# A spectral filter and a gated MLP summed on one core: another layout for the filtered products, and another route for the final sums

## The chip, the core and the metric

The kernel runs on one core of a Trainium2 chip. A core has a matrix engine (TensorE, PE in the profile, with its weight loads shown apart as PEld), a vector engine (VectorE, DVE), a scalar engine (ScalarE, ACT), a general engine (GpSimd, POOL) and a queue that only issues transfers here (SyncE, SP). They run side by side and wait for each other through semaphores. On-chip data lie in SBUF (128 partitions); TensorE writes its results to PSUM, eight banks of 512 float32 per partition, from which VectorE or ScalarE must copy them before a bank can be used again. The metric is the device time of one execution in microseconds (us).

## The reference

```python
x  = A_x                                   # 1 x 2048 x 640, bf16
xn = layernorm(x)
# A: spectral filter
X  = rfft2(xn.astype(float32))             # over 2048 and 640
yA = irfft2(X * (w_r + 1j * w_i), s=(2048, 640)).astype(bf16)   # w: 2048 x 321
# B: gated MLP without a nonlinearity
g  = xn @ w_gate                           # 640 -> 1536
u  = xn @ w_up
yB = (g * u) @ w_down                      # 1536 -> 640
out = x + yA + yB
```

## The kernel before

A small list scheduler in the kernel orders tasks for every engine ahead of time, with estimates of their durations; each engine then runs a fixed list in order, with semaphore waits between the lists. TensorE has three long stages in a row: the products g and u (L978 and L998 in the profile) interleaved first with the forward transform along 2048, then with the filter, and at the end the product with w_down (L1237).

**The filter.** There are 32 steps q. In each, a matmul (L1079, "C") finishes the forward transform of a group of rows into a PSUM bank; VectorE multiplies it by the real and by the imaginary part of the filter weights ("WM": two instructions of L1094 and one of L1097); another engine makes a negated copy of one half ("NG": L1106 on ScalarE, L1107 on VectorE or GpSimd); GpSimd arranges the rest ("NS": L1114 to L1116); ten matmuls ("IA": L1130 and L1131) take 128-column slices of these products as their weights and start the inverse transform. The frequencies are treated in classes, k = 0 to 3 for those of a residue modulo 10 and its mirror (h), and a fifth for the multiples of 5.

```python
# WM: psum (k h m) times weights (m k, ten apart), for the real and the imaginary weights (w)
for h in range(2):
    xh = ps[:, bk, 0:256].rearrange("p (k h m) -> p h m k", k=4, h=2)[:, h]
    wv = wg[:, :, 0:320].rearrange("p w (m k) -> p w m k", k=10)
    wv = wv[:, :, :, 1:5] if h == 0 else wv[:, :, :, 9:5:-1]
    dst = yg[:, 578:1090].rearrange("p (w h m k) -> p h w m k", w=2, h=2, k=4)[:, h]
    c.e.tensor_tensor(dst, xh.unsqueeze(1).to_broadcast([128, 2, 32, 4]), wv, _OP.mult)   # L1094
...
# NG: negated copy of the imaginary products
yg[:, 322:578]  <-  -1.0 * yg[:, 834:1090]
...
# IA
for k in range(5):
    if k < 4:
        l1, l2 = yg[:, 578 + k:1090:4], yg[:, 322 + k:834:4]
    else:
        l1, l2 = yg[:, 0:128], yg[:, 128:256]
    dst = ps[:, bk, 64 * k:64 * k + 64]
    c.e.matmul(dst, l1, v_ti[:, q, 0, :], start=True, stop=False)        # L1130
    ins = c.e.matmul(dst, l2, v_ti[:, q, 1, :], start=False, stop=True)  # L1131
# eIA: 320 sums from PSUM to SBUF, on ScalarE or VectorE (L718 / L719)
```

In the products' buffer the four classes k lie next to each other, element by element: VectorE writes them in one run, and the 128 columns that TensorE loads as weights for one class are four elements (8 bytes) apart.

**The end.** For each of 16 row tiles a, in two halves of 320 columns, twelve matmuls with w_down (L1237) and one that closes the inverse transform (L1249, "IV") add up in one PSUM bank. Beside it, for each pair of tiles, five small matmuls per tile ("I", L1159), a copy from PSUM, and a chain of thirteen VectorE instructions ("V", L1183 to L1216) prepare what IV multiplies. Then:

```python
def em_f1(c, ...):      # FIN, L1257: PSUM + residual -> output buffer, bf16
    return c.e.tensor_tensor(v_out[:, a % 2, sl3], ps[:, bk, 0:320], v_xr[:, xs, sl3], _OP.add)
f1 = T("FIN_%d_%d" % (a, hf), "dve", ..., frees=own, after=[iv])      # frees the bank
dma("st_out%d_%d" % (a, hf), ov[:, a, sl3], v_out[:, a % 2, sl3], ...) # a store per half
```

The last tile is cut in three (320, 192, 128 columns). The small copies that ScalarE and VectorE share (L718, L719) are one helper, so one line has many shapes.

Of the kernel before, what the change touches and what calls it, by code (L numbers as in the profile page):

```python
# [495 lines left out]
_ACTF = mybir.ActivationFunctionType  # L496
# [28 lines left out]
def _d_dve_psum(n):  # L525
    return n * 1.04 + 82.0
# [24 lines left out]
def _build(nc, A_x, A_w_r, A_w_i, B_w_gate, B_w_up, B_w_down, out, opts=None):  # L551
# [3 lines left out]
    with es:  # L555
# [147 lines left out]
        def bank_of(t):  # L703
            return t.units[1]
# [321 lines left out]
        for t in range(16):  # L1026
# [46 lines left out]
            for g in range(2):  # L1073
                q = 2 * t + g
                pg = pq + 0.0005 * g
                ys = 2 * yr + g

                def em_c(c, q=q, g=g, ar=ar):
                    return c.e.matmul(ps[:, bank_of(c.t), 0:_LP], v_tf[:, q, :], v_a[:, ar, 324 * g:324 * g + _LP],  # L1079
                                      start=True, stop=True)  # L1080
                tc = T("C_%d" % q, "pe", _d_mm(_LP), em_c, reads=[(b_a, ("r", 2 * ar, 2 * ar + 2)), (b_tf, ("t", t, t + 1))],
                       prio=pg, bank="single", cls="b")

                def em_wm(c, tc=tc, yr=yr, wr=wr, q=q, g=g):
                    bk = bank_of(tc)
                    o_ = 321 * (q % _WQ)
                    wg = v_wr[wr][:, :, o_:o_ + 321]
                    yg = v_y[:, yr, g]
                    for h in range(2):
                        xh = ps[:, bk, 0:256].rearrange("p (k h m) -> p h m k", k=4, h=2)[:, h]  # L1090
                        wv = wg[:, :, 0:320].rearrange("p w (m k) -> p w m k", k=10)
                        wv = wv[:, :, :, 1:5] if h == 0 else wv[:, :, :, 9:5:-1]
                        dst = yg[:, 578:1090].rearrange("p (w h m k) -> p h w m k", w=2, h=2, k=4)[:, h]
                        c.e.tensor_tensor(dst, xh.unsqueeze(1).to_broadcast([128, 2, 32, 4]), wv, _OP.mult)  # L1094
                    x5 = ps[:, bk, 256:321].unsqueeze(1).to_broadcast([128, 2, 65])
                    d5 = yg[:, 0:512].rearrange("p (w n) -> p w n", w=2)[:, :, 0:65]
                    return c.e.tensor_tensor(d5, x5, wg[:, :, 0:321:5], _OP.mult)  # L1097
                wm = T("WM_%d" % q, "dve", 895.0, em_wm,
                       reads=[(b_wr[wr][0], ("r", b_wr[wr][1], b_wr[wr][1] + 16))],
                       writes=[(b_y, ("r", 4 * ys, 4 * ys + 1))], prio=pg - 0.001, frees=tc)  # L1100
                hold(tc, wm)

                def em_ng(c, yr=yr, g=g):
                    yg = v_y[:, yr, g]
                    if c.e is nc.scalar:
                        return c.e.activation(yg[:, 322:578], yg[:, 834:1090], _ACTF.Copy, scale=-1.0)  # L1106
                    return c.e.tensor_scalar(yg[:, 322:578], yg[:, 834:1090], -1.0, None, _OP.mult)  # L1107
                T("NG_%d" % q, opts.get("ng_eng", ('pool', 'act', 'dve')),
                  {"act": _d_act(256), "dve": _d_dve_ts16(256), "pool": 900.0}, em_ng,
                  reads=[(b_y, ("r", 4 * ys, 4 * ys + 1))], writes=[(b_y, ("r", 4 * ys + 1, 4 * ys + 2))], prio=pg - 0.001)  # L1110

                def em_ns(c, yr=yr, g=g):
                    yg = v_y[:, yr, g]
                    c.e.tensor_copy(yg[:, 65:128], yg[:, 257:320])  # L1114
                    c.e.tensor_copy(yg[:, 193:256], yg[:, 1:64])  # L1115
                    return c.e.tensor_scalar(yg[:, 128:193], yg[:, 256:321], -1.0, None, _OP.mult)  # L1116
                T("NS_%d" % q, "pool", 700.0, em_ns,
                  reads=[(b_y, ("r", 4 * ys, 4 * ys + 1))], writes=[(b_y, ("r", 4 * ys + 2, 4 * ys + 3))], prio=pg - 0.001)

                def em_ia(c, q=q, yr=yr, g=g):  # L1120
                    bk = bank_of(c.t)
                    ins = None
                    yg = v_y[:, yr, g]
                    for k in range(5):
                        if k < 4:
                            l1, l2 = yg[:, 578 + k:1090:4], yg[:, 322 + k:834:4]
                        else:
                            l1, l2 = yg[:, 0:128], yg[:, 128:256]
                        dst = ps[:, bk, 64 * k:64 * k + 64]
                        c.e.matmul(dst, l1, v_ti[:, q, 0, :], start=True, stop=False)  # L1130
                        ins = c.e.matmul(dst, l2, v_ti[:, q, 1, :], start=False, stop=True)  # L1131
                    return ins
                ia = T("IA_%d" % q, "pe", 10 * _d_mm(64), em_ia,
                       reads=[(b_y, ("r", 4 * ys, 4 * ys + 3)), (b_wd, ("e", 128 * q, 128 * q + 128))],
                       prio=pg, bank="single", cls="b")

                def em_eia(c, ia=ia, t=t, g=g):
                    src = ps[:, bank_of(ia), 0:320].rearrange("p (k a m) -> p k a m", k=5, a=16)
                    return copy_on(c, v_z2w[:, :, :, t, 4 * g:4 * g + 4], src)
                eia = T("eIA_%d" % q, ("act", "dve"), {"dve": _d_dve_psum(320), "act": _d_act(320)}, em_eia,  # L1140
                        writes=[(b_z2, ("t", q, q + 1))], prio=pg - 0.001, frees=ia)
                hold(ia, eia)
# [78 lines left out]
        for a in range(16):  # L1221
# [5 lines left out]
            for hf, (c0, c1) in enumerate(pieces):  # L1227
                rb = [("r", 640 * (a % 2) + c0, 640 * (a % 2) + c1)]
                sl3 = slice(c0, c1)
                cuts = (0, 5, 9, 12) if a < opts.get("acc_split", 16) else (0, 12)  # L1230
                own = ag2 = None
                for k0, k1 in zip(cuts[:-1], cuts[1:]):
                    def em_ag2(c, a=a, sl3=sl3, k0=k0, k1=k1, own=own):
                        bk = bank_of(c.t) if own is None else bank_of(own)
                        ins = None
                        for ft in _FT_ORDER[k0:k1]:
                            ins = c.e.matmul(ps[:, bk, 0:sl3.stop - sl3.start], v_ht[:, ft, a * 128:(a + 1) * 128],  # L1237
                                             v_wd[:, ft, sl3], start=(ft == _FT_ORDER[0]), stop=False)
                        return ins
                    kw = dict(bank="single", cls="acc") if own is None else dict(after=[ag2])  # L1240
                    fts = _FT_ORDER[k0:k1]
                    rd = [(b_wd, ("e", 640 * min(fts), 640 * (max(fts) + 1)))] if k1 - k0 < 12 else [(b_wd, None)]
                    ag2 = T("ACC_%d_%d_%d" % (a, hf, k0), "pe", (k1 - k0) * _d_mm(c1 - c0), em_ag2,
                            reads=[(b_ht, ("col", a, a + 1))] + rd,
                            prio=pc + 0.01 + 0.001 * hf + opts.get("acc0_prio", 0.0) * (a < opts.get("acc_split", 16)), **kw)
                    own = own or ag2

                def em_iv(c, own=own, a=a, sl3=sl3):
                    return c.e.matmul(ps[:, bank_of(own), 0:sl3.stop - sl3.start], v_sm[:, 2, :], v_v[:, a, sl3],  # L1249
                                      start=False, stop=True)  # L1250
                iv = T("IV_%d_%d" % (a, hf), "pe", _d_mm(c1 - c0), em_iv,
                       reads=[(b_v, ("a", a, a + 1)), (b_sm, ("t", 1, 3))],
                       prio=opts.get("iv_prio", 5.0) + 0.05 * a + 0.01 + 0.001 * hf, after=[ag2])

                def em_f1(c, own=own, a=a, xs=xs, sl3=sl3):
                    bk = bank_of(own)
                    return c.e.tensor_tensor(v_out[:, a % 2, sl3], ps[:, bk, 0:sl3.stop - sl3.start], v_xr[:, xs, sl3],  # L1257
                                             _OP.add)
                f1 = T("FIN_%d_%d" % (a, hf), "dve", _d_dve_psum(c1 - c0), em_f1,
                       reads=[(b_xr, ("r", xs, xs + 1))], writes=[(b_out, rb[0])],  # L1260
                       prio=opts.get("fin_prio", 41.0) + 0.05 * a - 0.001, frees=own, after=[iv])
                dma("st_out%d_%d" % (a, hf), ov[:, a, sl3], v_out[:, a % 2, sl3], 128 * 2 * (c1 - c0), [],
                    prio=pc - 0.003, reads=[(b_out, rb[0])], semkey=("out", a % 2, hf))

        sch.window = 100.0
        sch.urgent = opts.get("urgent", ('T0_0', 'T0_1', 'T0_2', 'T0_3', 'sd_1', 'sd_2', 'sd_3'))
# [83 lines left out]
```

## Time and profile before

| | |
|---|---|
| time, median of 3 runs | 204.33 us (204.27 to 204.45) |
| span of the profiled execution | 202.8 us |
| granted TensorE clock in every stretch asked for | 1.00 |
| final sums on VectorE (L1257, 320 columns) | 31 times, 483 ns each |
| copies by ScalarE of 128x320 from PSUM | 25 times, 436 ns each |
| products of the filter (L1094) | 64 times, 416 ns each |
| stores of the output | 31, of 80 KB in the median |

How to read it: the profile gives each engine's busy time in us and as a share of the span, and groups instructions by line, shapes and engine. A duration is that of one instruction from start to end; neighbours overlap, so the distance from one start to the next is shorter (the two L1094 of a step take 0.76 us together, not 0.83). TensorE's matmul ends are modelled, so a busy TensorE is not proof of a full one: distances between starts are the better measure. "Idle before" names the engine whose semaphore ended a wait.

### The profile page before, as it was taken

How to read it: one execution, taken by the hardware profiler on the slowest of the kernel's cores; microseconds unless marked ns; L12 is line 12 of the kernel's file. 1: busy time of each engine (PE TensorE's matmuls, PEld its weight loads, DVE VectorE, ACT ScalarE, POOL GpSimd, SP SyncE). 2: the span in 40 equal slices, each digit the busy share in tenths (PEclk: the TensorE clock that was granted, in tenths of full speed). 3: DMA queues.
4: the chain of work that ended last, by engine and by line, in shares of the span. 5: the costliest groups of instructions: out<-in, count | busy, mean ns of one | idle time of the engine just before them, and what ended most of it. 6: DMA issues, size and time to landing. Idle time of an engine off the chain costs nothing.

```text
span 202.8 us, 4769 instructions
## 1 busy us (share of the span) xinstructions
PE 198.0 (98%) x1785; PEld 128.1 (63%) x1785; DVE 179.5 (89%) x511; ACT 127.5 (63%) x277; POOL 32.0 (16%) x108
## 2 busy tenths in 40 slices
PE   7999999999999999899999999999999999999995
PEld 7987644454444555556666666667777767777774
DVE  3599999999999997697988898864999999999983
ACT  3678899999975776869999999987611220200000
POOL 0000000000000000075754675453000000000000
DMA  6999983031161597605354444004313332332222
GB/s 183 300 341 378 377 80 65 3 65 32 32 63 39 112 276 194 197 14 132 74 145 114 103 102 127 0 5 136 92 32 97 106 107 66 113 90 81 93 65 65
DMA packets 31542, 23.82 MB, mean 117 GB/s; under 512 B 10528, under 2 KB 29472, under 8 KB 31392
## 3 DMA queue, kind: packets, MB, share of 16 engines
q1 hardware_dynamic: 30720, 23.16, 43.5%
q10 hardware_dynamic: 800, 0.36, 0.6%
q8 instruction: 14, 0.23, 0.5%
q14 instruction: 8, 0.07, 0.1%
HBM read 18.92 MB, written 2.62 MB: 106 GB/s over the span
## 4 chain that ended last, share of the span: by engine, by line
PE 85%; DVE 5%; SPq 4%; DMA 4%; issue 1%; ACT 1%
PE ps L978 44%; PE ps L1237 23%; SPq L712 4%; DMA arena<-in_A_x_dram 4%; PE ps L1131 3%; PE ps L1130 3%; PE ps L998 2%; PE ps L1079 2%; PE ps L938 2%; PE ps L1159 2%; PE ps L1249 2%; PE ps L1056 2%; DVE arena L719 1%; DVE arena L1257 1%; DVE arena L1186 0%
## 5 line engine op out<-in xcount | busy, mean ns | idle before, releaser
L718 ACT ACTIVATE arena<-ps 128x512 bf16<-128x512 f32 (+7 forms) x206 | 104.8, 547 | 40.1 <-PE ps L1159 24.0
L978 PE MATMUL ps<-arena 128*128 128x512 bf16 x420 | 97.0, 379 | 0.1
L978 PEld LDWEIGHTS ps<-arena 128*128 128x128 bf16 x420 | 38.9, 98 | 41.9 <-ACT arena L718 1.4
L1237 PE MATMUL ps<-arena 128*128 128x320 bf16 (+2 forms) x396 | 56.5, 295 | 0.2 <-DVE arena L1257 0.2
L1237 PEld LDWEIGHTS ps<-arena 128*128 128x128 bf16 x396 | 37.6, 98 | 13.9 <-DVE arena L1257 0.5
L1094 DVE TENSOR_TENSOR arena<-ps,arena 128x256 bf16<-128x256 f32 x64 | 24.0, 416 | 0.1
L1014 DVE TENSOR_TENSOR arena<-arena 128x512 bf16<-128x512 bf16 x42 | 17.7, 421 | 4.7 <-ACT arena L718 4.7
L1107 POOL TENSOR_SCALAR arena<-arena 128x256 bf16<-128x256 bf16 x8 | 6.8, 855 | 89.3 <-DVE arena L1097 89.2
L719 DVE CAST arena<-ps 64x321 bf16<-64x321 f32 (+1 forms) x25 | 12.2, 490 | 6.3 <-PE ps L1131 5.8
L1257 DVE TENSOR_TENSOR arena<-ps,arena 128x320 bf16<-128x320 f32 (+2 forms) x33 | 15.4, 473 | 1.8 <-PE ps L1249 1.8
L998 PE MATMUL ps<-arena 128*128 128x128 bf16 (+1 forms) x160 | 14.4, 246 | 0.4 <-ACT arena L718 0.4
L1130 PEld LDWEIGHTS ps<-arena 128*128 128x128 bf16 x160 | 12.4, 114 | 2.8 <-ACT arena L718 0.4
L998 PEld LDWEIGHTS ps<-arena 128*128 128x128 bf16 x160 | 12.0, 98 | 2.1 <-ACT arena L718 1.2
L1130 PE MATMUL ps<-arena 128*128 128x64 bf16 x160 | 13.3, 196 | 0.0
L1131 PE MATMUL ps<-arena 128*128 128x64 bf16 x160 | 13.3, 197 | 0.0
L1131 PEld LDWEIGHTS ps<-arena 128*128 128x128 bf16 x160 | 11.2, 113 | 2.1
L1116 POOL TENSOR_SCALAR arena<-arena 128x65 bf16<-128x65 bf16 x32 | 12.1, 378 | 0.0
L1114 POOL COPY arena<-arena 128x63 bf16<-128x63 bf16 x32 | 8.6, 268 | 17.1 <-DVE arena L1097 17.0
L1097 DVE TENSOR_TENSOR arena<-ps,arena 128x130 bf16<-128x130 f32 x32 | 9.3, 292 | 0.0
L776 ACT ACTIVATE arena<-arena 128x640 bf16<-128x640 bf16 x11 | 9.1, 824 | 0.0
L1115 POOL COPY arena<-arena 128x63 bf16<-128x63 bf16 x32 | 9.0, 280 | 0.0
L891 DVE TENSOR_TENSOR arena<-arena 128x384 f32<-128x384 bf16 x16 | 8.8, 552 | 0.0
(62 smaller groups left out, 221.0 us busy)
## 6 DMA issues: line engine op xcount, KB each, us to landing
arena<-in_A_x_dram SPq DMA_DIRECT2D x20, 160.0 KB, 2.4
out_dram<-arena SPq DMA_DIRECT2D x31, 80.0 KB, 1.6
arena<-in_A_w_r_dram SPq DMA_DIRECT2D x8, 160.5 KB, 3.0
arena<-in_A_w_i_dram SPq DMA_DIRECT2D x8, 160.5 KB, 3.0
arena<-in_B_w_gate_dram SPq DMA_DIRECT2D x4, 320.0 KB, 5.8
arena<-in_A_x_dram SPq DMA_DIRECT2D x1, 1280.0 KB, 9.8
arena<-in_A_w_r_dram SPq DMA_DIRECT2D x14, 80.2 KB, 2.9
arena<-in_A_w_i_dram SPq DMA_DIRECT2D x14, 80.2 KB, 3.1
```

Of the source, the lines that this page charges most:

```text
L718: return c.e.activation(dst, src, _ACTF.Copy)
L719: return c.e.tensor_copy(dst, src)
L978: ins = c.e.matmul(ps[:, bk, :], v_gw[:, w, j, ft, :], v_xt[:, j, rows], start=(j == 0), stop=(j == 4))
L998: ins = c.e.matmul(ps[:, bk, w * n:(w + 1) * n], v_gw[:, w, j, ft, :], v_xt[:, j, rows], start=(j == 0), stop=(j == 4))
L1014: return c.e.tensor_tensor(v_ht[:, ft0, rows], v_gbf[:, rr, 0, :], v_gbf[:, rr, 1, :], _OP.mult)
L1094: c.e.tensor_tensor(dst, xh.unsqueeze(1).to_broadcast([128, 2, 32, 4]), wv, _OP.mult)
L1097: return c.e.tensor_tensor(d5, x5, wg[:, :, 0:321:5], _OP.mult)
L1116: return c.e.tensor_scalar(yg[:, 128:193], yg[:, 256:321], -1.0, None, _OP.mult)
L1130: c.e.matmul(dst, l1, v_ti[:, q, 0, :], start=True, stop=False)
L1131: ins = c.e.matmul(dst, l2, v_ti[:, q, 1, :], start=False, stop=True)
L1237: ins = c.e.matmul(ps[:, bk, 0:sl3.stop - sl3.start], v_ht[:, ft, a * 128:(a + 1) * 128], v_wd[:, ft, sl3], start=(ft == _FT_ORDER[0]), st ...
L1257: return c.e.tensor_tensor(v_out[:, a % 2, sl3], ps[:, bk, 0:sl3.stop - sl3.start], v_xr[:, xs, sl3], _OP.add)
```

## The change

Two parts.

The products of the filter are stored class by class. A class has its own block of 192 elements: 64 negated imaginary products, 64 real ones, 64 imaginary ones. The 128 columns that one weight load takes are then one run. VectorE's instruction still goes through the elements in the same order (k fastest), so its consecutive results are now 192 elements, 384 bytes, apart. The negated copy reads and writes four runs of 64.

In the end stage, for tiles 0 to 14, ScalarE copies each half from PSUM to the output buffer as bf16, which frees the bank; when both halves are there, VectorE adds the residual in place with one bf16 instruction over 640 columns, and one store takes the whole tile. Tile 15 keeps the old way. This is to relieve VectorE in the end stage, and to halve the stores.

```diff
-                        dst = yg[:, 578:1090].rearrange("p (w h m k) -> p h w m k", w=2, h=2, k=4)[:, h]
+                        dst = yg[:, 322:1090].rearrange("p (k s h m) -> p h s m k", k=4, s=3, h=2)[:, h, 1:3]
                         c.e.tensor_tensor(dst, xh.unsqueeze(1).to_broadcast([128, 2, 32, 4]), wv, _OP.mult)
 ...
+                    yk = yg[:, 322:1090].rearrange("p (k s n) -> p s k n", k=4, s=3)
-                        return c.e.activation(yg[:, 322:578], yg[:, 834:1090], _ACTF.Copy, scale=-1.0)
-                    return c.e.tensor_scalar(yg[:, 322:578], yg[:, 834:1090], -1.0, None, _OP.mult)
+                        return c.e.activation(yk[:, 0], yk[:, 2], _ACTF.Copy, scale=-1.0)
+                    return c.e.tensor_scalar(yk[:, 0], yk[:, 2], -1.0, None, _OP.mult)
 ...
-                            l1, l2 = yg[:, 578 + k:1090:4], yg[:, 322 + k:834:4]
+                            b0 = 322 + 192 * k
+                            l1, l2 = yg[:, b0 + 64:b0 + 192], yg[:, b0:b0 + 128]
 ...
+                if a >= opts.get("fin_direct", 15):
+                    ...                       # FIN and its store as before
+                    continue
+                def em_f0(c, own=own, a=a, sl3=sl3):
+                    return copy_on(c, v_out[:, a % 2, sl3], ps[:, bank_of(own), 0:sl3.stop - sl3.start])
+                f0 = T("FINA_%d_%d" % (a, hf), opts.get("fin_eng", "act"), ..., frees=own, after=[iv])
+                if hf == 0:
+                    continue
+                def em_f2(c, a=a, xs=xs):
+                    return c.e.tensor_tensor(v_out[:, a % 2], v_out[:, a % 2], v_xr[:, xs, :], _OP.add)
+                T("FIN_%d" % a, "dve", _d_dve_tt16(640), em_f2, ...)
+                dma("st_out%d" % a, ov[:, a, :], v_out[:, a % 2], 128 * 1280, ...)
```

More of the change, by code (lines that the diff above doesn't have):

```diff
@@ L1253, in _build @@
                        prio=opts.get("iv_prio", 5.0) + 0.05 * a + 0.01 + 0.001 * hf, after=[ag2])
[L1255 to L1261, printed above, removed]
@@ L1262, in _build, with em_f1 @@
-                dma("st_out%d_%d" % (a, hf), ov[:, a, sl3], v_out[:, a % 2, sl3], 128 * 2 * (c1 - c0), [],
-                    prio=pc - 0.003, reads=[(b_out, rb[0])], semkey=("out", a % 2, hf))
+                if a >= opts.get("fin_direct", 15):
+                    def em_f1(c, own=own, a=a, xs=xs, sl3=sl3):
+                        bk = bank_of(own)
+                        return c.e.tensor_tensor(v_out[:, a % 2, sl3], ps[:, bk, 0:sl3.stop - sl3.start], v_xr[:, xs, sl3],
+                                                 _OP.add)
+                    f1 = T("FIN_%d_%d" % (a, hf), "dve", _d_dve_psum(c1 - c0), em_f1,
+                           reads=[(b_xr, ("r", xs, xs + 1))], writes=[(b_out, rb[0])],
+                           prio=opts.get("fin_prio", 41.0) + 0.05 * a - 0.001, frees=own, after=[iv])
+                    dma("st_out%d_%d" % (a, hf), ov[:, a, sl3], v_out[:, a % 2, sl3], 128 * 2 * (c1 - c0), [],
+                        prio=pc - 0.003, reads=[(b_out, rb[0])], semkey=("out", a % 2, hf))
+                    continue
@@ new lines, in em_f0 @@
+                def em_f0(c, own=own, a=a, sl3=sl3):
+                    return copy_on(c, v_out[:, a % 2, sl3], ps[:, bank_of(own), 0:sl3.stop - sl3.start])
+                f0 = T("FINA_%d_%d" % (a, hf), opts.get("fin_eng", "act"), {"act": _d_act(c1 - c0), "dve": _d_dve_psum(c1 - c0)}, em_f0,
+                       writes=[(b_out, rb[0])], prio=opts.get("fin_prio", 41.0) + 0.05 * a - 0.001, frees=own, after=[iv])
+                if hf == 0:
+                    continue
+                ro = [("r", 640 * (a % 2), 640 * (a % 2) + 640)]
@@ new lines, in em_f2 @@
+                def em_f2(c, a=a, xs=xs):
+                    return c.e.tensor_tensor(v_out[:, a % 2], v_out[:, a % 2], v_xr[:, xs, :], _OP.add)
+                T("FIN_%d" % a, "dve", _d_dve_tt16(640), em_f2, reads=[(b_xr, ("r", xs, xs + 1))],
+                  writes=[(b_out, ro[0])], prio=opts.get("fin_prio", 41.0) + 0.05 * a - 0.001)
+                dma("st_out%d" % a, ov[:, a, :], v_out[:, a % 2], 128 * 1280, [],
+                    prio=pc - 0.003, reads=[(b_out, ro[0])], semkey=("out", a % 2, 0))
```

## The prediction

> **What bounds the kernel now.** I read the page first: its busy shares, and the chain of work that ended last.
>
> ```profile
> PE 198.0 (98%) x1785; PEld 128.1 (63%) x1785; DVE 179.5 (89%) x511; ACT 127.5 (63%) x277; POOL 32.0 (16%) x108
> ...
> PE 85%; DVE 5%; SPq 4%; DMA 4%; issue 1%; ACT 1%
> ```
>
> TensorE carries 85% of the chain. Its ends are modelled, so I checked with distances between starts in the timeline: a 512-column matmul follows the one before after 216 ns, a 320-column one after 136 ns, nearly without exception. Adding up what exceeds these paces after 23 us gives about 1.5 us of real gaps: 0.70 us at 84.2, 0.31 at 93.2, 0.24 at 139.8, 0.34 at 163.3, and crumbs. So no relief of another engine can bring more than about 1.5 us; to bring more, a matmul must get shorter.
>
> Next, the busy time by stretch:
>
> ```profile
> 100.00:120.00 20.00, 20.00 (x253) 12.64 (x252) 17.12 (x54) 19.20 (x46) 11.76 (x40) 1.00 0.45 114
> ...
> 160.00:180.00 20.00, 19.82 (x158) 14.27 (x157) 20.00 (x51) 2.60 (x4) 0.00 (x0) 1.00 0.31 92
> ```
>
> The columns after the length are PE, PEld, DVE, ACT, POOL. In the filter stage (first line) VectorE has 2.9 us in 20 free; in the end stage (second line) it has none and ScalarE is empty. That is what the second part of the change looks at. But TensorE is dense in both.
>
> Then the groups with their shapes kept apart:
>
> ```profile
> L1094 DVE TENSOR_TENSOR arena<-ps,arena 128x256 bf16<-128x256 f32 x64 | 24.0, 416 | 0.1
> ...
> L1257 DVE TENSOR_TENSOR arena<-ps,arena 128x320 bf16<-128x320 f32 x31 | 14.8, 483 | 1.1 <-PE ps L1249 1.1
> ...
> L1130 PEld LDWEIGHTS ps<-arena 128*128 128x128 bf16 x160 | 12.4, 114 | 2.8 <-ACT arena L718 0.4
> ...
> L1097 DVE TENSOR_TENSOR arena<-ps,arena 128x130 bf16<-128x130 f32 x32 | 9.3, 292 | 0.0
> ...
> L1056 PEld LDWEIGHTS ps<-arena 128*128 128x128 bf16 x160 | 6.5, 98 | 0.7 <-issue 0.2
> ```
>
> L1130 loads weights 8 bytes apart in four of five classes and takes 114 ns; L1056 loads runs and takes 98. L1094 is 24 us of VectorE, all in the filter stage.
>
> Last, VectorE's timeline over one period of that stage (four steps, 6.75 us, repeated from 96.8 to 130.5):
>
> ```profile
> 110.41 0.75 DVE L1094 TENSOR_TENSOR arena<-ps,arena 128x256 bf16<-128x256 f32 x2
> 111.08 0.28 DVE L1097 TENSOR_TENSOR arena<-ps,arena 128x130 bf16<-128x130 f32 x1
> ...
> 112.16 0.75 DVE L1094 TENSOR_TENSOR arena<-ps,arena 128x256 bf16<-128x256 f32 x2
> 112.82 0.30 DVE L1097 TENSOR_TENSOR arena<-ps,arena 128x130 bf16<-128x130 f32 x1
> 113.03 0.43 DVE L1014 TENSOR_TENSOR arena<-arena 128x512 bf16<-128x512 bf16 x1
> 113.38 0.25 DVE L1107 TENSOR_SCALAR arena<-arena 128x256 bf16<-128x256 bf16 x1
> 113.55 0.99 DVE L719 CAST arena<-ps 64x321 bf16<-64x321 f32 x2
> 115.49 0.49 DVE L719 CAST arena<-ps 128x320 bf16<-128x320 f32 x1 [0.95 <-PE ps L1131]
> ```
>
> The only slack per period is the 0.95 us before the eIA copy; the other 5.78 us are work.
>
> **What the Trainium skill says.** "Vector Engine (DVE) Microarchitecture Reference", section "Measured stream behaviour on trn2", says a port keeps 1.04 ns per column only while consecutive elements come in runs of at least two adjacent 4-byte words; a destination that hops at every element cost 1.71 ns, and one that steps 24 words each time 2.50. That was measured with 4-byte elements. The change makes L1094's destination hop 384 bytes at every 2-byte element. The trace of before has no such destination. It does show that hopping reads aren't always paid: L1094 reads PSUM 256 bytes apart and L1097 reads weights 10 bytes apart, and both run at full rate (416 ns for 256 columns, as the contiguous sums of L1192 with 415; 292 for 130 columns, as a contiguous 128-column L1257 with 291). "Advanced Engine Details and Errata", section "Memory Cachelines", names a penalty when each SBUF access goes to another 16-byte line, which leans the same way. "TensorE: Matmul & The Clock Gate", section "Weight-path perf modes", allows strided columns in a fast load without naming a cost; here they cost 17 ns of load and, in starts, 4.0 ns per matmul (33.2 against 29.2 for the fifth, contiguous class).
>
> **The change part by part.** The instruction orders of both kernels agree on all engines until about 150 us; only shapes differ. So the filter stage keeps its order and the end stage gets a new one.
>
> 1. Weight loads: 4 of 5 classes, 256 matmuls, 4.0 ns each: −1.0 us on TensorE, on the path as long as TensorE is the bound there.
>
> 2. L1094. At 1.71 ns: 256 x 0.67 = +0.17 us each, +0.34 per step, 64 x 0.17 = 10.9 us in all. By occupancy a period asks for 5.78 + 8 x 0.17 = 7.15 us in 6.75: at least +0.4. By the chain it's more. Follow the period above: the fourth WM ends at 113.12, and later by 4 x 0.34 = 1.37. GpSimd's last NS for it (L1116) ends at 114.58 and would end at 115.95. The IA of that step starts at 115.29 now, 0.71 after NS; the smallest such distance in the trace is 0.22, so it would start at 116.17, 0.88 late. The next C matmul stands right behind this IA in TensorE's list, the next WM begins 0.34 after that C, and so the whole period moves by 0.88 each time. Steps 6 to 31 are 6.5 periods: 5.7 us. The first six steps have VectorE full already (6.83 busy of the 7.00 us from 83 to 90) and take 6 x 0.34 = 2.0. Sum: +7.8 us. Part 1 is then worth only some 0.3 of its 1.0, as TensorE has waits.
>
> 3. Negated copy: four runs of 64 instead of one of 256; taken as no change (417 ns on ScalarE, 252 on VectorE, 856 on GpSimd).
>
> 4. End stage: per pair of tiles four L1257, 0.40 us apart when dense, become two bf16 sums over 640. L1014, bf16 over 512, is followed by the next instruction after 0.34 us; scaled, 0.41. VectorE gains 1.6 − 0.8 = 0.8 us in each 7.06 us. ScalarE gets four copies of 436 ns, 1.7 us, where it has 1.3 us of work. But 7.06 us is 52 matmuls x 136 ns: TensorE sets the period, so this brings only its gaps at 163.3 and 164.3, about 0.4 us.
>
> 5. Stores: 31 become 18. They are issued off the path; the last, of 128 columns, stays as it is, and so do the 1.9 us from its issue at 200.84 to the end of the span.
>
> Sum: 204.3 + 7.8 − 0.3 − 0.4 = 211.4.
>
> **The rivals.** A: the hop costs nothing for 2-byte results, perhaps because a write is as easily absorbed as the hopping reads. Then 204.3 − 1.0 − 0.4 = 202.9. For it speak the two hopping reads at full rate; against it, the measurement that the page has for destinations alone. B: the hop costs what the 24-word step cost, 2.50 ns: +0.37 per instruction, +0.75 per step; the fourth WM is 3.0 late and the period 2.5 longer, 6.5 x 2.5 + 4.5 − 0.7 = +20, thus 224. The order here (four hops, then back beside the first) is more like the region-hopping case, so I hold it the less likely. C: the stage absorbs most of the 1.37 per period (slack of 0.95 on VectorE, other orders of arrival), only the occupancy excess of 0.4 counts: 6.5 x 0.4 + 2.0 − 0.7 = +3.9, thus 208. D: ScalarE becomes a new wait in the end stage, its final copies standing ahead of the copies that feed V. With 3.0 us of work in 7.06 that is worth a few tenths at most.
>
> **The range and the chances.** I give A 0.24, C or a smaller penalty 0.2, the main line 0.36, steeper ones up to B 0.2. The point sits between C and the main line at 210.5; 202.7 holds A, 219 leaves out the upper part of B. Faster by over 2% would need 200.2, beyond all that the gaps and the weight loads together hold (1.5 + 1.0): 0.02. Within 2% (to 208.4) fall A and most of C: 0.33. Slower: 0.65.
>
> **What would show it.** L1094's mean: 590 ns for the main line, 416 for A, near 790 for B. In the filter stage, waits of TensorE before L1130's successor and before C, VectorE busy near 100%, a period of 7.6 us instead of 6.75. The weight loads of IA at 98 to 100 ns and 29 ns between their starts hold part 1 right in any case. In the end stage VectorE drops below 100% and TensorE keeps 136 ns. It is wrong if L1094 stays at 416 ns, or if the period stretches much less than the chain says.

## Result and the profile after

The changed kernel takes 251.56 us (median of 4 runs, 251.14 to 251.78) where the kernel before takes 204.39 us: a ratio of 1.230, 95% interval 1.228 to 1.232. The direction was predicted; the size was not: +47 us against +6, far outside the range.

The profile of the changed kernel first, busy shares and the chain that ended last, by engine and by line:

```profile
PE 211.8 (85%) x1785; PEld 129.8 (52%) x1785; DVE 226.1 (91%) x496; ACT 141.2 (57%) x307; POOL 32.7 (13%) x108
...
PE 53%; DVE 35%; issue 4%; DMA 3%; SPq 3%; POOL 1%; ACT 1%; POOLq 0%
DVE arena L1094 27%; PE ps L978 23%; PE ps L1239 21%; DVE arena L719 4%; DMA arena<-in_A_x_dram 3%; SPq L712 3%; PE ps L998 2%; PE ps L1161 2%; PE ps L938 2%; PE ps L1251 2%; DVE arena L1014 2%; DVE arena L1097 2%; PE ps L1056 1%; PE ps L1132 1%; POOL arena L1117 0%
```

VectorE went from 5% of the chain to 35%, and one line, L1094, makes 27% of the span. The groups by shape (busy us, mean ns of one, idle time before and what ended it) say what became of it:

```profile
L1094 DVE TENSOR_TENSOR arena<-ps,arena 128x256 bf16<-128x256 f32 x64 | 78.2, 1413 | 1.7 <-PE ps L1079 1.7
...
L1097 DVE TENSOR_TENSOR arena<-ps,arena 128x130 bf16<-128x130 f32 x32 | 16.1, 503 | 0.0
...
L1132 PE MATMUL ps<-arena 128*128 128x64 bf16 x160 | 14.9, 201 | 24.0 <-ACT arena L718 11.8 <-POOL arena L1117 10.5 <-DVE arena L1097 1.4
...
L1132 PEld LDWEIGHTS ps<-arena 128*128 128x128 bf16 x160 | 12.0, 103 | 34.7 <-ACT arena L718 17.5 <-issue 8.8 <-DVE arena L1014 3.2
...
L1278 DVE TENSOR_TENSOR arena<-arena 128x640 bf16<-128x640 bf16 x15 | 7.3, 487 | 3.5 <-ACT arena L718 3.4
```

L1094 was 416 ns and is 1413, and of this instruction the change alters the destination alone: it reads the same operands in the same order. L1097, which the change doesn't touch, went from 292 to 503: it follows two L1094 and seems to wait for their results to be written. TensorE's matmuls stand idle for 24.0 us before IA (L1132 now, L1130 before, where it was 0.0), and its weight loads for 34.7 us (2.8 before). VectorE's timeline over three of the four steps of a period in the filter stage, up to the next product:

```profile
133.83 2.46 DVE L1094 TENSOR_TENSOR arena<-ps,arena 128x256 bf16<-128x256 f32 x2
135.91 0.49 DVE L1097 TENSOR_TENSOR arena<-ps,arena 128x130 bf16<-128x130 f32 x1
136.32 2.44 DVE L1094 TENSOR_TENSOR arena<-ps,arena 128x256 bf16<-128x256 f32 x2
138.38 0.49 DVE L1097 TENSOR_TENSOR arena<-ps,arena 128x130 bf16<-128x130 f32 x1
138.80 2.42 DVE L1094 TENSOR_TENSOR arena<-ps,arena 128x256 bf16<-128x256 f32 x2
140.86 0.50 DVE L1097 TENSOR_TENSOR arena<-ps,arena 128x130 bf16<-128x130 f32 x1
141.27 0.40 DVE L1014 TENSOR_TENSOR arena<-arena 128x512 bf16<-128x512 bf16 x1
141.60 0.26 DVE L1108 TENSOR_SCALAR arena<-arena 128x256 bf16<-128x256 bf16 x1
141.78 1.51 DVE L719 CAST arena<-ps 64x321 bf16<-64x321 f32 x3
143.21 2.45 DVE L1094 TENSOR_TENSOR arena<-ps,arena 128x256 bf16<-128x256 f32 x2
```

A step (two L1094 and L1097) takes 2.48 us from start to start where it took 0.87. The wait before the eIA copy is gone: between steps 10 and 26 VectorE is idle for less than 0.05 us in a period, where it was 0.95, and a period of four steps is 12.2 us instead of 6.75.

From the starts in the trace: from the first C matmul to the last IA matmul 101.4 us against 54.2 (+47.2); everything before it +0.15; everything after it 63.05 against 63.47 (−0.4). The whole loss lies in the filter stage. TensorE's granted clock falls there too, which the stretches show (PE, PEld, DVE, ACT, POOL, then the clock):

```profile
100.00:120.00 20.00, 13.92 (x141) 7.87 (x139) 17.60 (x29) 9.75 (x22) 6.01 (x20) 0.83 0.23 57
...
200.00:220.00 20.00, 20.00 (x167) 14.87 (x166) 19.67 (x46) 8.38 (x18) 0.00 (x0) 1.00 0.33 102
```

Where TensorE waits, some twenty matmuls of 512 columns are followed by the next after 427 ns instead of 216. Whether that adds to the time is taken up below.

### The profile page after: what moved, and what is told of

Its sections match the earlier page's. It is cut to its first block, busy times and chain, and to the rows that moved or that the text cites. A ratio compares the mean times of both kernels' runs of the same rounds, so it can differ in the third digit from the quotient of the medians.

```text
span 249.7 us, 4768 instructions
## 1 busy us (share of the span) xinstructions
PE 211.8 (85%) x1785; PEld 129.8 (52%) x1785; DVE 226.1 (91%) x496; ACT 141.2 (57%) x307; POOL 32.7 (13%) x108
## 4 chain that ended last, share of the span: by engine, by line
PE 53%; DVE 35%; issue 4%; DMA 3%; SPq 3%; POOL 1%; ACT 1%; POOLq 0%
DVE arena L1094 27%; PE ps L978 23%; PE ps L1239 21%; DVE arena L719 4%; DMA arena<-in_A_x_dram 3%; SPq L712 3%; PE ps L998 2%; PE ps L1161 2%; PE ps L938 2%; PE ps L1251 2%; DVE arena L1014 2%; DVE arena L1097 2%; PE ps L1056 1%; PE ps L1132 1%; POOL arena L1117 0%
## 5 line engine op out<-in xcount | busy, mean ns | idle before, releaser
L718 ACT ACTIVATE arena<-ps 128x512 bf16<-128x512 f32 (+7 forms) x236 | 117.8, 533 | 57.8 <-PE ps L1251 29.6
L978 PE MATMUL ps<-arena 128*128 128x512 bf16 x420 | 104.0, 398 | 6.8 <-DVE arena L1097 6.7
L1094 DVE TENSOR_TENSOR arena<-ps,arena 128x256 bf16<-128x256 f32 x64 | 78.2, 1413 | 1.7 <-PE ps L1079 1.7
L978 PEld LDWEIGHTS ps<-arena 128*128 128x128 bf16 x420 | 40.2, 101 | 53.6 <-DVE arena L1097 8.5
L1239 PEld LDWEIGHTS ps<-arena 128*128 128x128 bf16 x396 | 37.7, 98 | 13.5
L1132 PE MATMUL ps<-arena 128*128 128x64 bf16 x160 | 14.9, 201 | 24.0 <-ACT arena L718 11.8
L1132 PEld LDWEIGHTS ps<-arena 128*128 128x128 bf16 x160 | 12.0, 103 | 34.7 <-ACT arena L718 17.5
L1107 ACT ACTIVATE arena<-arena 128x256 bf16<-128x256 bf16 x16 | 6.7, 417 | 40.1 <-DVE arena L1097 40.1
L1097 DVE TENSOR_TENSOR arena<-ps,arena 128x130 bf16<-128x130 f32 x32 | 16.1, 503 | 0.0
L1115 POOL COPY arena<-arena 128x63 bf16<-128x63 bf16 x32 | 9.3, 290 | 50.9 <-DVE arena L1097 50.9
L1133 PE MATMUL ps<-arena 128*128 128x64 bf16 x160 | 14.9, 202 | 0.0
L719 DVE CAST arena<-ps 64x321 bf16<-64x321 f32 (+1 forms) x25 | 12.2, 490 | 2.6 <-PE ps L1133 2.0
L998 PEld LDWEIGHTS ps<-arena 128*128 128x128 bf16 x160 | 12.0, 98 | 2.4 <-ACT arena L718 1.4
L1117 POOL TENSOR_SCALAR arena<-arena 128x65 bf16<-128x65 bf16 x32 | 12.2, 381 | 0.0
L1133 PEld LDWEIGHTS ps<-arena 128*128 128x128 bf16 x160 | 11.8, 104 | 0.7 <-issue 0.5
L1278 DVE TENSOR_TENSOR arena<-arena 128x640 bf16<-128x640 bf16 x15 | 7.3, 487 | 3.5 <-ACT arena L718 3.4
L1056 PE MATMUL ps<-arena 128*128 128x64 bf16 (+1 forms) x160 | 8.6, 200 | 1.7 <-DVE arena L1097 1.7
```

The source lines that it names most:

```text
L718: return c.e.activation(dst, src, _ACTF.Copy)
L719: return c.e.tensor_copy(dst, src)
L978: ins = c.e.matmul(ps[:, bk, :], v_gw[:, w, j, ft, :], v_xt[:, j, rows], start=(j == 0), stop=(j == 4))
L998: ins = c.e.matmul(ps[:, bk, w * n:(w + 1) * n], v_gw[:, w, j, ft, :], v_xt[:, j, rows], start=(j == 0), stop=(j == 4))
L1056: ins = c.e.matmul(ps[:, bk, k * 64:k * 64 + n], v_uq[:, k, t, :], v_fd[:, k * 128 + w * n: k * 128 + w * n + n], start=True, stop=True)
```

## The experiments

Theory at the start: the results of L1094 that land 384 bytes apart cost VectorE about 4 ns each, VectorE thereby sets the pace of the filter stage, and the second part of the change is harmless. Rivals: the end stage or the lowered clock have a share; it is the layout and not the order of writing; the distance of 384 bytes is special.

In what follows "apart" is the median distance from one start on VectorE to the next, and "period" is the mean time of four steps, a quarter of the time from the C matmul of step 10 to that of step 26, both from the trace. A kernel whose time stands without a ratio was timed in one run.

### One part at a time

The layout alone, with final sums and stores as before:

```diff
-                if a >= opts.get("fin_direct", 15):
+                if a >= opts.get("fin_direct", 0):
```

> The first part of the change alone: class-by-class layout, final sums and stores as before. Theory (hopping writes): VectorE's product instruction pays about 4.2 ns per element because its destination hops 384 bytes at each element; this alone carries the whole loss, so 251 to 253 us, L1094 near 1.4 us, filter stage about 101 us instead of 54. Rival (the two parts add, the end stage or the lowered TensorE clock carry a good part): clearly under 245 us.

Measured 251.47 us, ratio 1.227 (1.224 to 1.231); L1094 1415 ns; filter stage 101.4 us. All of the loss is in the first part.

The final sums alone (products, negated copy and weight loads as in the kernel before):

```diff
-  dst = yg[:, 322:1090].rearrange("p (k s h m) -> p h s m k", ...)[:, h, 1:3]   # after
+  dst = yg[:, 578:1090].rearrange("p (w h m k) -> p h w m k", ...)[:, h]         # as before
```

> The second part alone: products laid out as before, final sums by ScalarE, one store per tile. Theory: TensorE sets the period of the end stage (52 matmuls of 136 ns for two tiles), so only its gaps of some 0.4 us can be won: 203.7 to 204.4 us. Rival (ScalarE's copies and the in-place sum put a new wait on the path): above 205 us.

Measured 204.38 us against 204.74, ratio 0.9975 (0.9967 to 0.9983). A second time, beside other kernels further down:

> The final sums by ScalarE alone once more, on the same chip as the two above: 0.4 to 0.6 us below the kernel before.

204.41 against 204.69 us, ratio 0.9979 (0.9970 to 0.9988). A small gain, of 0.3 to 0.5 us. In the end stage of this kernel, by stretches (same columns as above):

```profile
160.00:180.00 20.00, 20.00 (x161) 14.72 (x160) 19.70 (x46) 7.41 (x16) 0.00 (x0) 1.00 0.32 100
180.00:202.00 22.00, 20.38 (x163) 15.04 (x161) 15.49 (x37) 4.38 (x10) 0.00 (x0) 1.00 0.25 76
```

In the kernel before, VectorE was busy 20.00 us of the first stretch and 19.01 of the second. It is relieved by 3.5 us in the second and the kernel hardly notices, since TensorE was dense: only its gaps at 163 and 164 us, some 0.4 us in all, are gone.

### The order of writing

The changed layout, but each class's 32 elements in a row before the next class:

```diff
-  xh = ps[...].rearrange("p (k h m) -> p h m k", k=4, h=2)[:, h]
-  wv = wg[:, :, 0:320].rearrange("p w (m k) -> p w m k", k=10)
-  dst = yg[:, 322:1090].rearrange("p (k s h m) -> p h s m k", ...)[:, h, 1:3]
+  xh = ps[...].rearrange("p (k h m) -> p h k m", k=4, h=2)[:, h]
+  wv = wg[:, :, 0:320].rearrange("p w (m k) -> p w k m", k=10)
+  dst = yg[:, 322:1090].rearrange("p (k s h m) -> p h s k m", ...)[:, h, 1:3]
```

> The changed kernel with one difference: the product instruction goes through a class's 32 elements first and through the classes after, so its results are written in runs of 32; PSUM is then read in runs too, and the filter weights 20 bytes apart. Layout, negated copy, weight loads and end stage stay as changed. Theory (hopping writes are the cause): L1094 back to about 416 ns and the time to 202.5 to 203.5 us, below before, as the weight loads keep their gain of 1.0 us. Rival 1 (the hop only moves to the weights, a read step of 20 bytes costs like the page's source hop, 1.73 ns): L1094 near 590 ns, 207 to 212 us. Rival 2 (it was the layout itself, not the order of writing): still near 250 us.

210.60 us, ratio 1.027 (1.026 to 1.029). In the same layout, the order of writing was what cost 4 ns an element, and rival 1 of this run is right as well: now the filter weights are read 20 bytes apart.

```profile
L1094 DVE TENSOR_TENSOR arena<-ps,arena 128x256 bf16<-128x256 f32 x64 | 36.4, 613 | 0.2 <-PE ps L1079 0.2
...
L1132 PEld LDWEIGHTS ps<-arena 128*128 128x128 bf16 x160 | 11.0, 97 | 10.1 <-ACT arena L1107 4.3 <-ACT arena L718 2.9 <-DVE arena L1108 0.9
```

L1094s are 0.52 us apart instead of 0.33: 0.19 / 256 = 0.74 ns more per element, thus about 1.8 in all. That agrees with the 1.73 ns that the Trainium skill, "Vector Engine (DVE) Microarchitecture Reference", section "Measured stream behaviour on trn2", gives for one source hopping at every element ("the page" below). The weight loads show what the layout was made for: 97 ns, and their matmuls 29 ns apart.

The same loop order in the layout of before, where the destination then steps 8 bytes:

```diff
-  dst = yg[:, 578:1090].rearrange("p (w h m k) -> p h w m k", ...)[:, h]
+  dst = yg[:, 578:1090].rearrange("p (w h m k) -> p h w k m", ...)[:, h]   # xh, wv as in the run above
```

> The kernel before with the same loop order as the run above: its destination then steps 8 bytes per element, its weights 20. Theory a (every write that is not adjacent to the last costs its own access, whatever the distance): L1094 near 1.3 us, time near 250 us. Theory b (only leaving a 16-byte line costs, here every second element): about half of the loss, L1094 near 0.7 to 0.8 us. Theory c (short steps are free): L1094 near 416 ns, time near 204.4 us.

214.55 us; L1094 773 ns, 0.54 and 0.59 us apart. That is the size that theory b names, but the reads 20 bytes apart alone account for 613 ns, as the run above shows. How the costs of reads and writes add up is not shown, so what follows for the destination is a bound: at steps of 8 bytes an element costs at most half of what it costs at a hop of 384. Theory a is out.

### Distance, and what a hop carries

Class blocks 200 elements apart instead of 192:

```diff
-  b0 = 322 + 192 * k
+  b0 = 322 + 200 * k        # dst and the negated copy likewise
```

> The changed kernel with the class blocks 200 elements apart instead of 192, so the destination hops 400 bytes. Theory (it is the hop itself, at whatever distance): L1094 stays at about 1.4 us, time 250 to 252 us. Rival (384 bytes is three times 128, and the hops fall on the same part of memory): 400 bytes is cheaper, L1094 nearer 0.6 us, the time under 225 us.

248.9 us, L1094 1385 ns. And 128 bytes:

```diff
+  dst = yg[:, 578:1090].rearrange("p (w k h m) -> p h w m k", ...)[:, h]
+  l1, l2 = yg[:, 578 + 128 * k:706 + 128 * k], yg[:, 322 + 128 * k:450 + 128 * k]
   ...   # negated copy as in the kernel before
```

> Final sums as changed; products in the old three blocks (negated, real, imaginary), each block class by class, so the destination hops 128 bytes at each element, in the same loop order as before and after. The weight loads take contiguous columns, which are then not those of one class: the result isn't the reference's, the work is the same. Theory (hop at whatever distance): L1094 about 1.4 us, time 250 us. Rival (cost grows with the distance): well under 1 us and under 230 us.

250.75 us, L1094 1409 ns. The distance of 384 bytes is not special. Next, how much a hop carries: runs of four neighbours before each hop (r=4), one instruction for each of real and imaginary weights.

```diff
+  for w in range(2):
+      xh = ps[...].rearrange("p (k h m r) -> p h m k r", k=4, h=2, r=4)[:, h]
+      wv = wg[:, w, 0:320].rearrange("p (m r k) -> p m k r", k=10, r=4)   # then classes 1:5 or 9:5:-1
+      dst = yg[:, 322:1090].rearrange("p (k s h m r) -> p h s m k r", ...)[:, h, 1 + w]
```

> The changed layout written in runs of four neighbours (8 bytes) before the hop of 384 bytes; four instructions of 128 elements per step instead of two of 256. Theory (a fixed cost of about 4.2 ns per hop, hidden when four elements share it): what remains is the read step of 20 bytes at about 1.8 ns, 128 x 1.8 + 75 = 0.3 us from start to start, 1.2 us for the four where the kernel with runs of 32 needs 1.05; time 212 to 216 us. Rival (every write to the spread blocks costs, run or not): 0.6 us each, time near 250 us.

213.63 us, 0.29 us apart: as expected, what is left has the size of the reads. Then r=2:

> The changed layout written in runs of two neighbours (4 bytes) before each hop of 384 bytes, four instructions of 128 elements. Theory (4.2 ns per hop): 64 hops x 4.2 + 75 = 0.34 us from start to start, little above the 0.29 of the runs of four; time near 217 us. Rival (4.2 ns per element written into spread blocks, unless a longer run is there): 0.6 us, time near 250 us.

This broke the theory of a cost per hop. It takes 204.22 us (one run, beside 204.62), and the products in this kernel have

```profile
L1095 DVE TENSOR_TENSOR arena<-ps,arena 128x128 bf16<-128x128 f32 x128 | 28.5, 287 | 0.1
```

287 ns for 128 elements and 0.20 us apart, the pace of contiguous work (256 elements 0.33 us apart in the kernel before), although the destination hops 384 bytes at every second element. Not even the reads cost here: they alternate between two rows of weights 20 bytes apart and come back beside where they were.

So three more runs. Pairs shifted by one element, so that a pair doesn't lie as the pairs above (`322` becomes `323` throughout):

> The changed layout written in pairs, shifted by one element, so that a pair lies across two 4-byte words. Theory (a write of half a word costs about 4 ns when it stands alone): each pair is two such writes, 0.6 us from start to start for 128 elements, time near 250 us. Rival (what costs is a hop at every element, and pairs halve their number): 0.20 us, time near 204.2 us.

Hops of 16 bytes, in blocks of eight neighbours (dst `"p (w h m k r) -> p w h m r k"`, r=8), and of 64 bytes (dst `"p (w h k m) -> p h w m k"`), both with contiguous weight loads that take other columns than those of one class:

> Destination hopping 16 bytes at each element, inside blocks of 64 bytes, four instructions of 128 elements; the matmuls load contiguous columns, which are not those of one class. Theory (single half words cost 4.2 ns wherever they stand): 0.6 us from start to start, near 250 us. Rival (distance counts, as 8 bytes were cheap): 0.2 to 0.35 us, near 204 to 214 us.

> Destination hopping 64 bytes at each element, two instructions of 256 elements; the matmuls load contiguous columns, which are not those of one class. Theory (single half words cost 4.2 ns wherever they stand): near 1.1 us from start to start, near 250 us. Rival (distance counts): about 0.35 to 0.6 us, 204 to 215 us.

They took 222.12, 248.95 and 249.16 us. From the three profiles:

```profile
L1095 DVE TENSOR_TENSOR arena<-ps,arena 128x128 bf16<-128x128 f32 x128 | 51.3, 590 | 0.5 <-PE ps L1079 0.4
```

```profile
L1095 DVE TENSOR_TENSOR arena<-ps,arena 128x128 bf16<-128x128 f32 x128 | 75.3, 862 | 1.7 <-PE ps L1079 1.7
```

```profile
L1094 DVE TENSOR_TENSOR arena<-ps,arena 128x256 bf16<-128x256 f32 x64 | 76.9, 1392 | 1.4 <-PE ps L1079 1.4
```

The first is neither theory's: 0.36 us apart, not 0.20 and not 0.6. From 16 bytes on, the distance doesn't count. Put per visit of the destination to a place, with some 67 ns of fixed time taken off each instruction's distance (0.33 us for 256 elements without a penalty and 0.20 for 128 leave about 1.03 ns per element and 67 ns beside them):

| destination | apart, us | per visit |
|---|---|---|
| one element, hop 384 bytes | 1.15 (the second of two, 256 elements) | 4.2 ns |
| one element, hop 64 bytes | 1.12 (the same) | 4.1 ns |
| one element, hop 16 bytes | 0.55 (128 elements) | 3.8 ns |
| one element, step 8 bytes | 0.59 (256 elements) | at most 2.1 ns, or 4.1 per 16 bytes (its reads alone take 1.8 per element) |
| pair shifted by one, hop 384 bytes | 0.36 (64 pairs) | 4.6 ns |
| pair as first laid, hop 384 bytes | 0.20 (64 pairs) | at most 2.1 ns |

Within about a tenth, all six fit a rule that a visit which leaves a 4-byte word half written costs about 4.2 ns, once per 16 bytes, and one that fills its words does not. That alignment counts is shown: the last two rows differ in the shift of one element (and two elements more per buffer). The rest is argued from these rows, its "once per 16 bytes" from the fourth and fifth alone; a quarter of the shifted pairs lies across a boundary of 16 bytes, for which the rule as worded would ask 5.3 ns and not 4.6. Why any of it should be so, no run shows.

### What the weight loads are worth, and what can be kept

Products as before, final sums as changed, and the IA matmuls load contiguous columns, which are then not those of one class:

```diff
-  l1, l2 = yg[:, 578 + k:1090:4], yg[:, 322 + k:834:4]
+  l1, l2 = yg[:, 578 + 128 * k:706 + 128 * k], yg[:, 322 + 128 * k:450 + 128 * k]
```

> What the contiguous weight loads are worth when nobody pays for them: products written as before, final sums as changed, and the ten matmuls of a step load contiguous columns, which are then not those of one class (the result isn't the reference's). Theory: 256 matmuls x 4.0 ns = 1.0 us on a dense TensorE: 1.0 us below the kernel with the final sums alone, so 203.2 to 203.5 where that one has 204.4. Rival (the stage's waits swallow it): within 0.3 us of it.

203.68 us beside 204.69 for the kernel before (ratio 0.9952, 0.9938 to 0.9965) and 204.41 for the final sums alone: 0.7 us in the medians; the filter stage alone is 0.94 us shorter (53.27 against 54.20). That is the most that contiguous loads could bring here.

Classes stored in two pairs, every second element loaded:

```diff
+  for d in range(2):
+      xh = ps[...].rearrange("p (d k h m) -> p d h m k", d=2, k=2, h=2)[:, d, h]
+      ...   # wv: two of the four classes
+      dst = yg[:, 322:1090].rearrange("p (d s h m k) -> p d h s m k", d=2, s=3, h=2, k=2)[:, d, h, 1:3]
   ...
+  b0 = 322 + 384 * (k // 2) + k % 2
+  l1, l2 = yg[:, b0 + 128:b0 + 383:2], yg[:, b0:b0 + 255:2]
```

> A compromise with the reference's result: classes stored in two pairs (0 with 1, 2 with 3), so a weight load takes every second element; VectorE writes runs of 64 and reads the weights two by two; four instructions of 128 elements per step; final sums as changed. Theory: no hop on the writing side and only every second read hops, so L1094's successor runs at full rate, 128 x 1.04 + 75 = 0.21 us from start to start, 0.84 per step against 0.67; VectorE's slack of 0.95 us in four steps hides 0.7 of that but the first six steps pay 1.0 us; weight loads gain half of 1.0 us: 204 to 205 us, no better than the final sums alone. Rival (two-element runs still pay): over 207 us.

204.47 us, ratio 0.9990 (0.9981 to 1.0000). Loads every second element apart are as fast as contiguous ones (98 ns; matmuls 29 ns apart), better than expected; the period is 6.67 us. But two more instructions per step make the first ten steps 17.39 us instead of 17.01, and the last ones lose too. So the same with the old layout in the first six steps:

```diff
+  if q < 6:   # products, negated copy and weight loads as in the kernel before
```

> The pairs layout from the seventh step on, the old layout in the first six, where VectorE has no slack; final sums as changed. Theory: the six steps no longer pay 1.0 us, the steady part keeps its period of 6.67 us instead of 6.75 (0.5 us over six and a half periods): 203.6 to 204.0 us, about 0.9 us below the kernel before. Rival (the loss of the pairs layout lies elsewhere): no better than 204.4.

204.00 us against 204.62, ratio 0.9962 (0.9948 to 0.9976). And the changed kernel's own layout, written in pairs (r=2) from the seventh step on:

> The changed kernel with the products written in aligned pairs from the seventh step on, and the first six steps in the old layout. Theory: contiguous weight loads at no cost on VectorE's side, period 6.67 us: 203.7 to 204.1 us, 0.6 to 0.9 us below the kernel before. Rival: no better than the final sums alone, 204.4.

204.02 against 204.63 us, ratio 0.9961 (0.9946 to 0.9975). Both are 0.6 us below the kernel before, and the best found with the reference's result. About half of that is the final sums, which alone bring 0.3 to 0.5 us; the times of all three, as ratios, overlap in their intervals. The layout's own share shows in the filter stage, 53.93 us in both traces against 54.18 and 54.20 with the final sums alone.

## Why the prediction was wrong

**What bounds it, and the ceiling of the gain: right.** The final sums brought 0.3 to 0.5 us, against "about 0.4"; the weight loads, freed of their price, 0.7 to 0.9 against 1.0; the best kernel is 0.6 us faster.

**The failing term is in step 2, "At 1.71 ns: 256 x 0.67 = +0.17 us each".** The wait that it foresaw, VectorE's longer products, is the one that came; its size was wrong. It measured +0.58 for the first and +0.82 for the second L1094 of a step, and +0.21 for the L1097 behind them: +1.61 us per step, where the prediction had +0.34. Per element that is 4.2 ns against the 1.71 taken from the page and the 2.50 of rival B. With +1.61 per step in the prediction's own occupancy sum, the filter stage loses 5.46 us in each of 6.5 periods and 9.7 us in the first six steps, +45 us, of +47.2 measured. The page measured 4-byte elements and the prediction said so, but took the figure over to 2-byte ones and called 2.50 the steep end. The pairs don't contradict the page's 1.71: 4 bytes at a hop cost at most 2.1 ns. No run here has elements of 4 bytes. Of 2-byte results, the rivals said only that the hop might cost nothing; none said that halves of a word might be dearer.

**The way from VectorE to the time: the occupancy was right and the chain was not needed.** Step 2 gave two readings of a longer L1094: 5.78 us of work per period plus the addition (+0.4 over the 6.75), or, along the chain of one period, +0.88. Six kernels test it, five of them with a sum above 6.75 us. With x for the addition to one step, L1097 included:

| kernel | x, us | 5.78 + 4x | period measured, us |
|---|---|---|---|
| pairs stored together | 0.14 | 6.36 | 6.67 (VectorE idle for 0.39 of it) |
| runs of 32 | 0.38 | 7.32 | 7.31 |
| runs of 4 | 0.48 | 7.71 | 7.70 |
| 8-byte steps | 0.50 | 7.78 | 7.76 |
| shifted pairs | 0.76 | 8.83 | 8.81 |
| changed kernel | 1.61 | 12.21 | 12.20 |

In all five in which the sum passes the 6.75 us of before, VectorE's work is the period. The chain's 0.88 rested on GpSimd finishing 1.46 us after the fourth WM, as it does in the kernel before. There GpSimd is still at the third step's work, which its timeline shows (L1114 of the fourth step begins where L1116 of the third ends); in the kernel with runs of 32, the products come further apart, and GpSimd is found waiting:

```profile
116.94 0.38 POOL L1117 TENSOR_SCALAR arena<-arena 128x65 bf16<-128x65 bf16 x1
117.57 0.50 POOL L1115 COPY arena<-arena 128x63 bf16<-128x63 bf16 x1 [0.25 <-DVE arena L1097]
118.01 0.23 POOL L1116 COPY arena<-arena 128x63 bf16<-128x63 bf16 x1
118.21 0.38 POOL L1117 TENSOR_SCALAR arena<-arena 128x65 bf16<-128x65 bf16 x1
```

The fourth WM ends at 117.51 there, GpSimd at 118.59: 1.08 us. The queue that the chain carried along had gone with the slower arrival. Here the chain, walked with the queues of the kernel before, overstated a delay that thins them out. For the changed kernel itself this hardly matters: with +1.61 per step the two readings come to +45 and +48 us.

**The clock** has little part in the time. The changed kernel's steady period of 12.20 us is VectorE's work of 12.21, so that slower matmuls hide in TensorE's waits; in the runs of 32 and the shifted pairs the clock is 1.00 and the same sum holds. The slower matmuls do spoil one sign that the prediction named: IA weight loads at 98 ns with 29 ns between starts. In the changed kernel the means read 103 and 33 in spite of the contiguous layout (the median distance is 29), and only the kernels with contiguous loads in every step and TensorE at full clock show means of 97 to 98 and 29.

**Steps 3 to 5 and rival D: as predicted.** The negated copy stayed at 417 ns on ScalarE. The stores before are 33 and not 31, as two smaller ones of 48 and 32 KB come on top; nothing hangs on them. VectorE fell below 100% in the end stage and TensorE held its 136 ns. ScalarE's final copies make no wait on the path: in the changed kernel its 29.6 us of waiting are for TensorE's closing matmuls (L1251).

## What to carry to other kernels

Before reordering a buffer for the engine that reads it, look at the innermost order in which the other engine writes it: single bf16 results scattered over SBUF cost four times as much as a run here, 4.2 against 1.03 ns, and a hidden instruction became the bound. Scattered in aligned pairs, the results cost nothing but the two instructions more per step. Where an engine's work per period passed the bound engine's, its sum of start-to-start distances was the new period, in five kernels of five; the chain of waits of the kernel before was not.

## What the runs showed that was not expected

- The destination cost per visit: 4.1 to 4.2 ns for one bf16 element at hops of 64 to 400 bytes, 3.8 at 16, at most 2.1 for an aligned pair, 4.6 for a shifted one.
- The instruction behind is longer too: L1097, itself unchanged, takes 503 ns instead of 292 behind two scattered L1094.
- bf16 reads 20 bytes apart cost 1.8 ns per element when they go straight on, but nothing when they alternate between two rows and return to the neighbour (0.20 us apart for 128 elements).
- Weight loads of TensorE pay for columns 8 bytes apart (114 ns, matmuls 33 ns apart) and not for columns 4 bytes apart (98 ns, 29 ns).
